# Weight split of a top-k attention and gated feed-forward kernel: high halves and half of the fractions on GpSimd, word and fraction double-buffered

## The chip, the cores and the metric

The kernel runs on one NeuronCore of a Trainium2 chip. A core has five engines, each with its own queue that it works through in order: TensorE (PE in the rows; its weight loads are PEld), VectorE (DVE), ScalarE (ACT), GpSimd (POOL) and SyncE (SP), which here issues nearly all DMAs. They wait for each other through semaphores. The metric is the time of one execution on the device in microseconds.

## The reference

```python
scores = scale * np.matmul(q, k.transpose(0, 1, 3, 2))      # 8 batches, 8 heads, 576 x 576, head 64
kth = np.partition(scores, -top_k, axis=-1)[..., -top_k:-top_k + 1]   # top_k = 32
attn = softmax(np.where(scores >= kth, scores, -1e9))
x = np.matmul(attn, v)                                       # then heads side by side: 4608 x 512
gate = 1.0 / (1.0 + np.exp(-(x @ w_gate)))                   # 512 x 1536
out = (gate * (x @ w_val)) @ w_out                           # 1536 x 512
```

All inputs and the output are float32.

## The kernel before

Attention runs as a chain of 160 steps (batch, pair of heads, tile of 128 queries). In a step TensorE makes scores into PSUM (`pss`), ScalarE copies them to SBUF (`s`), VectorE finds candidates for the 32 largest of each row (`cand`, `tops`, `leads`, many short MAX instructions), ScalarE marks what lies under a bound (`under`, one buffer), GpSimd multiplies scores and marks (`u`, L356 and L357), VectorE takes the threshold out of `u` (`kths`, L366) and masks the exponentials with it (`e`, L292, two SBUF operands). TensorE then transposes `e` and weighs the values. Of finished tokens the feed-forward part makes its products; it takes each matrix as a high part, rounded to TensorE's shorter float, and the rest, and multiplies three times.

For that the weights are split once, in the first 200 us, while the first attention steps run: `split_weights` takes 18 tiles of 128 x 1024 words. The inputs are 64-bit floats, so a tile is read as pairs of 32-bit words, `low` and `top`, each at every second word of `raw`. For each tile: two DMAs load `raw` (two buffers); ScalarE makes `lead` and `minus_zero` out of `top` (L151, L152); VectorE puts them together to a float (L153), masks sign and exponent into `top` (L161) and makes the fraction `frac` out of `low` and `top` (L162); ScalarE rounds `lead` to the high half of the weight tile (`w_split` in the rows, L163). TensorE adds up, for each half tile, `lead`, minus the high half, and `frac` (`wrest`, L168 to L170, in this order), ScalarE rounds the sum to the low half (L171), and a DMA stores the tile for later. Of these, `lead`, `frac` and `minus_zero` have one buffer each.

The order of instructions on each engine is laid out when the program is built, by a scheduler that goes by costs of its own; `run` hands it the steps and interleaves the split with them (`HELD`, `SOON`, `RUSH` say how many tiles after how many steps). On the chip the order is fixed.

Of the kernel before, what the change touches and what calls it, by code (L numbers as in the profile page):

```python
# [11 lines left out]
F32 = mybir.dt.float32  # L12
# [5 lines left out]
AF = mybir.ActivationFunctionType  # L18
ALU = mybir.AluOpType
# [11 lines left out]
def tile_topk_attention_then_gated_ffn(  # L31
# [10 lines left out]
    nc = tc.nc  # L42
# [72 lines left out]
    def split_weights():  # L115

        W = 2 * NP * P
        with ExitStack() as pre:
            signs, raws, parts = [
                pre.enter_context(tc.tile_pool(name=n, bufs=bufs, reuse_waits="tile"))  # L120
                for n, bufs in (("signs", 1), ("raw", 2), ("parts", 1))
            ]
            minus_zero = signs.tile([P, W, 2], F16, tag="minus_zero", name="minus_zero")
            nc.gpsimd.memset(minus_zero.bitcast(U32), 0)
            plus, minus = [signs.tile([P, P], F32R, tag=t, name=t) for t in ("plus", "minus")]
            nc.scalar.activation(plus, ident, AF.Copy)
            nc.scalar.activation(minus, ident, AF.Copy, scale=-1.0)
            todo = [x for g in range(NG) for x in (*range(g * FG, (g + 1) * FG), NF + 2 * g, NF + 2 * g + 1)]
            raw_of = {}

            def load_raw(idx):
                raw = raw_of[idx] = raws.tile([P, W, 2], U32, tag="raw", name=f"wraw_{idx}")
                for i in range(2):
                    half = slice(i * NP * P, (i + 1) * NP * P)
                    nc.sync.dma_start(raw[:, half].rearrange("p n t -> p (n t)"), w[idx][:, half].bitcast(U32))

            for idx in todo[:2]:
                load_raw(idx)
                yield
            for idx in todo:  # L140
                wt = pools["w"].tile([P, 2, 2, NP, P], F32R, tag="w", name=f"w_split_{idx}")
                if idx not in raw_of:
                    load_raw(idx)
                raw = raw_of.pop(idx)
                low, top = raw[:, :, 0], raw[:, :, 1]
                high, rests = [wt[:, :, x].rearrange("p i c n -> p i (c n)") for x in range(2)]
                lead = parts.tile([P, W], F32, tag="lead", name=f"wt_lead_{idx}")
                frac = parts.tile([P, W], F32R, tag="frac", name=f"wt_frac_{idx}")
                lead_u, sign = lead.bitcast(U32), top.bitcast(F32)
                with tc.issue_after(copies[1].ins):  # L150
                    nc.scalar.activation(lead, sign, AF.Copy, scale=2.0**-112)  # L151
                    nc.scalar.activation(minus_zero[:, :, 1], sign, AF.Copy, scale=2.0**-60)  # L152
                nc.vector.scalar_tensor_tensor(  # L153
                    lead_u,
                    lead_u,
                    3,
                    minus_zero.rearrange("p n t -> p (n t)").bitcast(U32),
                    op0=ALU.logical_shift_left,
                    op1=ALU.bitwise_or,
                )  # L160
                nc.vector.tensor_scalar(top, lead_u, 0xFF800000, None, op0=ALU.bitwise_and)  # L161
                nc.vector.scalar_tensor_tensor(frac, low, 2.0**-52, sign, op0=ALU.mult, op1=ALU.mult)  # L162
                nc.scalar.activation(high, lead.rearrange("p (i n) -> p i n", i=2), AF.Copy)  # L163
                yield
                for i in range(2):
                    half = slice(i * NP * P, (i + 1) * NP * P)
                    rest = ps_f.tile([P, NP * P], F32, tag="f", name=f"wrest_{idx}_{i}")
                    nc.tensor.matmul(rest, ident, lead[:, half], start=True, stop=False)  # L168
                    nc.tensor.matmul(rest, minus, high[:, i], start=False, stop=False)
                    nc.tensor.matmul(rest, plus, frac[:, half], start=False, stop=True)  # L170
                    nc.scalar.activation(rests[:, i], rest, AF.Copy)  # L171
                nc.sync.dma_start(w_split[idx], wt.rearrange("p i a c n -> p i a (c n)").bitcast(F32))
                if idx not in (*range(FG), NF, NF + 1):
                    fresh[idx] = wt
                yield
        pools["kraw"] = ctx.enter_context(tc.tile_pool(name="bkr2", bufs=2, reuse_waits="tile"))
        pools["ql"] = ctx.enter_context(tc.tile_pool(name="bql", bufs=3, reuse_waits="tile"))
        pools["x"] = ctx.enter_context(tc.tile_pool(name="bxc", bufs=NP, reuse_waits="tile"))
        pools["spare"] = ctx.enter_context(tc.tile_pool(name="late", bufs=1, reuse_waits="tile"))
# [337 lines left out]
    def run(general):  # L517
# [27 lines left out]
        if not general:  # L545
            ffn_pools()
            splits = split_weights()
# [176 lines left out]
```

## Time and profile before

| | |
|---|---|
| median of 3 runs | 1561.76 us (1561.25 to 1561.87) |
| profiled execution | 1560.76 us, its span 1558.9 us |
| busy share of the span | TensorE 97%, VectorE 84%, ScalarE 72%, GpSimd 65% |
| 18 weight tiles split | first instruction at 7.3 us, last store issued at 202.7 us |

The span is the time from the first to the last instruction of the profile; 1.86 us of the execution lie around it. A row of a group gives a count, the group's busy time, the mean length of one in ns, and the engine's idle time just before them with what ended it.

### The profile page before, as it was taken

The numbers are of one execution on the slowest core, as the hardware profiler recorded it, in microseconds if no ns is written. First come the engines' busy times: TensorE is split into PE (matmuls) and PEld (weight loads), VectorE is DVE, ScalarE is ACT, GpSimd is POOL, SyncE is SP. The second block draws the span as 40 slices with busy tenths as digits, with TensorE's granted clock in tenths as the row PEclk, the third lists the DMA queues.
The fourth block names the chain that finished last, engine by engine and source line by source line (L and its number), as shares of the span: only waits on it lengthen the run. The fifth ranks groups of instructions, "written<-read, shape, count | busy, mean of one in ns | idle before, by whom it ended". The sixth has DMA issues, their size and how long they took to land.

```text
span 1558.9 us, 33891 instructions
## 1 busy us (share of the span) xinstructions
PE 1514.1 (97%) x10586; PEld 1381.1 (89%) x10586; DVE 1310.2 (84%) x5966; ACT 1115.2 (72%) x2405; POOL 1019.9 (65%) x1596
## 2 busy tenths in 40 slices
PE   6889999999999999999999999999999999999998
PEld 2447689989999999999999999999999999999998
DVE  8999969989998889888988898998988798998311
ACT  8998968778776777777676777777766677777221
POOL 4556658877766766787566886788655786666211
PEclk9899999999999999999999999999999999999999
DMA  7663698877655665566655665565655565565574
GB/s 264 250 239 123 214 366 319 285 255 274 236 190 206 247 213 189 193 223 216 218 193 193 236 220 197 190 236 209 211 207 179 211 224 203 179 215 184 192 275 158
DMA packets 88895, 344.14 MB, mean 221 GB/s; under 512 B 9856, under 2 KB 36992, under 8 KB 57984
## 3 DMA queue, kind: packets, MB, share of 16 engines
q1 hardware_dynamic: 88560, 341.58, 61.8%
q8 instruction: 86, 1.41, 0.4%
q14 instruction: 105, 0.86, 0.2%
q10 hardware_dynamic: 144, 0.29, 0.0%
HBM read 313.52 MB, written 28.31 MB: 219 GB/s over the span
## 4 chain that ended last, share of the span: by engine, by line
PE 79%; DVE 10%; POOL 5%; ACT 2%; issue 2%; DMA 1%; POOLq 0%; DVEq 0%; ACTq 0%
PE pz L476 12%; PE pz L475 12%; PE pz L477 12%; PE pss L239 9%; PE pt L378 6%; PE po L414 6%; PE po L498 6%; PE po L497 6%; PE po L496 6%; DVE cand L338 2%; POOL u L356 2%; DVE e L292 2%; PE po L428 2%; DVE kths L366 2%; PE po L424 1%
## 5 line engine op out<-in xcount | busy, mean ns | idle before, releaser
L356 POOL TENSOR_TENSOR u<-s,under 128x288 f32<-128x288 f32 x576 | 451.5, 806 | 140.9 <-ACT under L350 132.2
L338 DVE MAX8 cand<-s 128x8 f32<-128x72 f32 x2304 | 350.7, 217 | 72.6 <-ACT s L246 64.5
L476 PE MATMUL pz<-xl,w 128*128 128x384 f32 (+1 forms) x1184 | 389.9, 330 | 1.4 <-POOL xl L448 1.4
L475 PE MATMUL pz<-xh,w 128*128 128x384 f32 (+1 forms) x1184 | 391.1, 332 | 0.0
L477 PE MATMUL pz<-xh,w 128*128 128x384 f32 (+1 forms) x1184 | 388.9, 329 | 0.0
L292 DVE SCALAR_TENSOR_TENSOR e<-s,kths,e 128x576 f32<-128x576 f32 x288 | 279.7, 976 | 5.6 <-ACT e L287 5.3
L350 ACT ACTIVATE under<-s,leads 128x576 bf16<-128x576 f32 x288 | 223.3, 776 | 75.5 <-DVE leads L342 35.7
L287 ACT ACTIVATE e<-s,st 128x576 f32<-128x576 f32 x288 | 210.1, 773 | 57.5 <-POOL st L346 56.7
L366 DVE MAX8 kths<-u 128x8 f32<-128x584 f32 x288 | 218.8, 760 | 32.8 <-POOL u L357 30.8
L483 POOL TENSOR_TENSOR gl<-gf,gh 128x384 fp32r<-128x384 f32 (+1 forms) x156 | 155.6, 998 | 123.2 <-ACT gh L482 117.0
L476 PEld LDWEIGHTS pz<-xl,w 128*128 128x128 f32 x1184 | 223.7, 189 | 2.5 <-POOL xl L448 2.2
L477 PEld LDWEIGHTS pz<-xh,w 128*128 128x128 f32 x1184 | 223.6, 189 | 0.3
L475 PEld LDWEIGHTS pz<-xh,w 128*128 128x128 f32 x1184 | 222.8, 189 | 0.8 <-issue 0.4
L379 ACT ACTIVATE et<-pt 128x384 f32<-128x384 f32 x384 | 176.7, 487 | 36.3 <-PE pt L378 34.6
L497 PE MATMUL po<-gl,w 128*128 128x384 f32 (+1 forms) x592 | 194.4, 329 | 0.6 <-POOL gl L483 0.5
L498 PE MATMUL po<-gh,w 128*128 128x384 f32 (+1 forms) x592 | 194.8, 330 | 0.0
L496 PE MATMUL po<-gh,w 128*128 128x384 f32 (+1 forms) x592 | 194.5, 333 | 0.1
L378 PE MATMUL pt<-ident,e 128*128 128x128 f32 x1152 | 176.6, 275 | 3.3 <-DVE e L292 2.0
L246 ACT ACTIVATE s<-pss 128x576 f32<-128x576 f32 x252 | 161.3, 640 | 22.0 <-PE pss L239 20.9
L239 PE MATMUL pss<-k,qh 128*128 128x288 f32 (+2 forms) x588 | 166.2, 301 | 1.9 <-ACT s L246 1.7
L239 PE MATMUL pss<-k,ql 128*128 128x288 f32 (+2 forms) x588 | 159.8, 294 | 0.0
L378 PEld LDWEIGHTS pt<-ident,e 128*128 128x128 f32 x1152 | 140.6, 141 | 17.5 <-issue 3.9
(108 smaller groups left out, 2901.9 us busy)
## 6 DMA issues: line engine op xcount, KB each, us to landing
w<-ws SPq DMA_DIRECT2D x222, 1024.0 KB, 4.9
v<-in_v_dram SPq DMA_DIRECT2D x68, 352.0 KB, 3.1
wraw<-in_w_dram SPq DMA_DIRECT2D x36, 512.0 KB, 4.5
ws<-w_split SPq DMA_DIRECT2D x18, 1024.0 KB, 4.3
qraw<-in_q_dram SPq DMA_DIRECT2D x140, 128.0 KB, 2.9
kraw<-in_k_dram SPq DMA_DIRECT2D x56, 288.0 KB, 4.5
out_dram<-acc SPq DMA_DIRECT2D x40, 192.0 KB, 5.1
out_dram<-acc SPq DMA_DIRECT2D x12, 128.0 KB, 5.5
```

Of the source, the lines that this page charges most:

```text
L239: nc.tensor.matmul(ps[:, half, o : o + n], x[:, h * P : (h + 1) * P], ks[h][:, k0 : k0 + n], start=t == 0, stop=t == len(todo) - 1,)
L292: nc.vector.scalar_tensor_tensor(e[:, j], s[:, j], kth[j], e[:, j], op0=ALU.is_ge, op1=ALU.mult, accum_out=st[:, 4 + j : 5 + j])
L338: nc.vector.max(cand[:, j, 8 * g : 8 * g + 8], s[:, j, g * SEG : (g + 1) * SEG])
L356: nc.gpsimd.tensor_tensor(u[:, j, part], s[:, j, part], under[:, j, part], op=ALU.mult)
L366: nc.vector.max(kths[:, n_tiles - col - j : n_tiles - col - j + 8], u[:, j])
L378: nc.tensor.transpose(pt[:, c], ef[:, k0 : k0 + P], ident)
L475: nc.tensor.matmul(ps, wt[:, u, 0, d], xh, start=d == 0, stop=False)
L476: nc.tensor.matmul(ps, wt[:, u, 0, d], xl, start=False, stop=False)
L477: nc.tensor.matmul(ps, wt[:, u, 1, d], xh, start=False, stop=d == NP - 1)
L496: nc.tensor.matmul(ps, wt[:, e % 2, 0, f], gh, start=f == 0, stop=False)
L497: nc.tensor.matmul(ps, wt[:, e % 2, 0, f], gl, start=False, stop=False)
L498: nc.tensor.matmul(ps, wt[:, e % 2, 1, f], gh, start=False, stop=f == FG - 1)
```

## The change

The rounding of `lead` to the high half moves from ScalarE to GpSimd, for all 18 tiles. For every second tile of the order in `todo`, the fraction is made in two instructions: ScalarE turns `low` into a scaled float in its own place (`part`), and GpSimd multiplies it by `sign`; VectorE has no part in it. `lead` and `frac` get two buffers. Lines behind the edit stand 8 further on in the rows of the changed kernel (L171 is L179 there, L292 is L300, L356 is L364), and the remaining fraction on VectorE is L167.

```diff
-                for n, bufs in (("signs", 1), ("raw", 2), ("parts", 1))
+                for n, bufs in (("signs", 1), ("raw", 2), ("parts", 2))
...
                 nc.vector.tensor_scalar(top, lead_u, 0xFF800000, None, op0=ALU.bitwise_and)
-                nc.vector.scalar_tensor_tensor(frac, low, 2.0**-52, sign, op0=ALU.mult, op1=ALU.mult)
-                nc.scalar.activation(high, lead.rearrange("p (i n) -> p i n", i=2), AF.Copy)
+                if todo.index(idx) % 2:
+                    part = low.bitcast(F32)
+                    nc.scalar.activation(part, low, AF.Copy, scale=2.0**-52)
+                    nc.gpsimd.tensor_tensor(frac, part, sign, op=ALU.mult)
+                else:
+                    nc.vector.scalar_tensor_tensor(frac, low, 2.0**-52, sign, op0=ALU.mult, op1=ALU.mult)
+                if True:
+                    nc.gpsimd.tensor_copy(high, lead.rearrange("p (i n) -> p i n", i=2))
+                else:
+                    nc.scalar.activation(high, lead.rearrange("p (i n) -> p i n", i=2), AF.Copy)
```

The scheduler lays out all five queues anew. Names in the rows below carry the step (tile and pair of heads) or a number of the build. First GpSimd's queue at the sixth weight tile, one of those with the fraction on GpSimd; before:

```order
L356 TENSOR_TENSOR u_0_1_394<-s_0_1_208,under_0_1_395 128x288 x2
L346 TENSOR_SCALAR st_0_2_626<-tops_0_2_625 128x2
L356 TENSOR_TENSOR u_0_1_394<-s_0_1_208,under_0_1_395 128x288 x2
L357 TENSOR_TENSOR u_0_1_394<-wanted,sums_0_1_392 128x2x8
L356 TENSOR_TENSOR u_1_1_497<-s_1_1_284,under_1_1_498 128x288 x4
L357 TENSOR_TENSOR u_1_1_497<-wanted,sums_1_1_495 128x2x8
L448 TENSOR_TENSOR xl_0_593<-rs_1_0_606,xh_0_592 128x256
L356 TENSOR_TENSOR u_0_2_629<-s_0_2_380,under_0_2_630 128x288 x4
L357 TENSOR_TENSOR u_0_2_629<-wanted,sums_0_2_627 128x2x8
```

And now, at the same attention steps:

```order
L169 CAST w_split_677<-wt_lead_681 128x2x512
L306 COPY inv_0_1_543<-st_0_1_392 128x128
L165 TENSOR_TENSOR wt_frac_682<-wraw_678 128x1024
L364 TENSOR_TENSOR u_0_2_631<-s_0_2_381,under_0_2_632 128x288 x2
L354 TENSOR_SCALAR st_1_2_732<-tops_1_2_731 128x2
L364 TENSOR_TENSOR u_0_2_631<-s_0_2_381,under_0_2_632 128x288 x2
L365 TENSOR_TENSOR u_0_2_631<-wanted,sums_0_2_629 128x2x8
```

The rounding (CAST, L169) and the fraction (L165) stand in the queue between the attention's tasks; `u_0_2` and the `st` after it come behind them.

VectorE's queue from this tile's mask (L161) on; before:

```order
L161 TENSOR_SCALAR wraw_676<-wt_lead_679 128x1024
L338 MAX cand_0_3_858<-s_0_3_615 128x8 x2
L344 MATCH_REPLACE cand_1_2_727<-tops_1_2_728,cand_1_2_727 128x64
L338 MAX cand_0_3_858<-s_0_3_615 128x8
L344 MATCH_REPLACE cand_1_2_727<-tops_1_2_728,cand_1_2_727 128x64
L366 MAX kths<-u_0_2_629 128x8
L338 MAX cand_0_3_858<-s_0_3_615 128x8
L295 TENSOR_SCALAR st_1_1_494<-st_1_1_494 128x2
L162 SCALAR_TENSOR_TENSOR wt_frac_680<-wraw_676 128x1024
```

And now:

```order
L161 TENSOR_SCALAR wraw_678<-wt_lead_681 128x1024
L374 MAX kths<-u_1_1_499 128x8
L352 MATCH_REPLACE cand_1_2_730<-tops_1_2_731,cand_1_2_730 128x64
L346 MAX cand_0_3_862<-s_0_3_617 128x8 x4
L350 MAX tops_1_2_731<-cand_1_2_730 128x8
L346 MAX cand_0_3_862<-s_0_3_617 128x8 x4
L448 TENSOR_TENSOR rs_1_0_608<-po_1_0_596,rs_1_0_608 128x256
L374 MAX kths<-u_1_1_499 128x8
L300 SCALAR_TENSOR_TENSOR e_1_1_498,st_1_1_496<-s_1_1_284,kths,e_1_1_498 128x576
```

The fraction (L162) is gone behind the mask of this tile; other searches for maxima and the masking `e_1_1` follow instead.

ScalarE's queue around the same tile; before:

```order
L163 ACTIVATE w_split_554<-wt_lead_558 128x2x512
L152 ACTIVATE minus_zero<-wraw_676 128x1024
L447 ACTIVATE xh_0_592<-rs_1_0_606 128x256
L270 ACTIVATE s_1_2_483<-pss_1_2_1_488 128x2x288
L151 ACTIVATE wt_lead_679<-wraw_676 128x1024
L379 ACTIVATE et_0_1_698<-pt_0_1_0_699 128x3x128
L350 ACTIVATE under_0_2_630,sums_0_2_627<-s_0_2_380,leads 128x576 x2
L171 ACTIVATE w_split_554<-wrest_0_566 128x512
L171 ACTIVATE w_split_554<-wrest_1_571 128x512
```

And now:

```order
L358 ACTIVATE under_1_1_500,sums_1_1_497<-s_1_1_284,leads 128x576
L151 ACTIVATE wt_lead_681<-wraw_678 128x1024
L152 ACTIVATE minus_zero<-wraw_678 128x1024
L164 ACTIVATE wraw_678<-wraw_678 128x1024
L278 ACTIVATE s_0_3_617<-pss_0_3_0_618 128x2x288
L387 ACTIVATE et_0_1_701<-pt_0_1_0_702 128x3x128
L179 ACTIVATE w_split_556<-wrest_0_568 128x512
L179 ACTIVATE w_split_556<-wrest_1_573 128x512
L444 ACTIVATE rs_1_0_608<-po_1_0_596 128x256
```

The rounding L163 is gone from the queue, and the float of the fraction (L164) follows the two copies out of `raw`.

## Rows read from the trace of the kernel before

**Rows 1.** The page's second part: busy tenths in 40 slices of 39 us.

```profile
PE   6889999999999999999999999999999999999998
...
DVE  8999969989998889888988898998988798998311
...
POOL 4556658877766766787566886788655786666211
```

**Rows 2.** Busy time by stage, microseconds and instructions; granted clock; DMA.

```profile
0.00:116.00 116.00, 86.57 (x372) 44.75 (x372) 108.82 (x453) 104.92 (x181) 57.85 (x92) 0.91 0.69 250
116.00:220.00 104.00, 97.70 (x631) 74.49 (x631) 86.22 (x334) 83.39 (x163) 59.51 (x88) 0.98 0.59 213
220.00:1440.00 1220.00, 1216.60 (x8882) 1152.06 (x8883) 1089.39 (x5123) 902.61 (x2014) 879.71 (x1390) 1.00 0.63 220
```

**Rows 3.** VectorE's groups from 0 to 116 us: count, busy, mean, idle before.

```profile
L292 DVE SCALAR_TENSOR_TENSOR e<-s,kths,e 128x576 f32<-128x576 f32 x18 | 16.1, 897 | 0.0
L162 DVE SCALAR_TENSOR_TENSOR wt_frac<-wraw 128x1024 fp32r<-128x1024 uint32 x11 | 15.2, 1384 | 0.0
L153 DVE SCALAR_TENSOR_TENSOR wt_lead<-wt_lead,minus_zero 128x1024 uint32<-128x1024 uint32 x11 | 13.9, 1266 | 0.0
...
L161 DVE TENSOR_SCALAR wraw<-wt_lead 128x1024 uint32<-128x1024 uint32 x11 | 7.7, 702 | 0.0
```

**Rows 4.** ScalarE's groups of the split, 0 to 116 us.

```profile
L151 ACT ACTIVATE wt_lead<-wraw 128x1024 f32<-128x1024 f32 x11 | 12.9, 1171 | 0.5 <-DMA wraw<-in_w_dram 0.5
...
L163 ACT ACTIVATE w_split<-wt_lead 128x1024 fp32r<-128x1024 f32 x10 | 10.8, 1083 | 2.4 <-DVE wt_lead L153 2.4
```

**Rows 5.** Waits from 0 to 205 us: total, times, longest.

```profile
PE pss L269 <- ACT s L270: 8.7, 9, 2.8
...
DVE kths L366 <- POOL u L357: 2.8, 4, 1.0
...
PE wrest L169 <- ACT w_split L163: 1.6, 2, 1.4
...
PE pz L476 <- POOL xl L448: 1.2, 1, 1.2
```

**Rows 6.** GpSimd's lines: shortest/median/longest ns; xl's first row is the whole trace, the rest to 205 us.

```profile
L448 POOL TENSOR_TENSOR xl<-rs,xh x84: 314/662/1787, 53.4 to 1468.8; 128x192 fp32r<-128x192 f32 x28, 128x64 fp32r<-128x64 f32 x20, 128x320 fp32r<-128x320 f32 x16, 128x384 fp32r<-128x384 f32 x12
...
L448 POOL TENSOR_TENSOR xl<-rs,xh x7: 718/739/1787, 53.4 to 203.7; 128x256 fp32r<-128x256 f32 x7
...
L298 POOL COPY inv<-st x18: 280/290/861, 27.4 to 203.0; 128x128 f32<-128x128 f32 x18
...
L356 POOL TENSOR_TENSOR u<-s,under x72: 722/734/1783, 14.5 to 190.6; 128x288 f32<-128x288 f32 x72
...
L357 POOL TENSOR_TENSOR u<-wanted,sums x20: 196/219/1194, 17.2 to 191.7; 128x16 f32<-128x16 f32 x16, 128x8 f32<-128x8 f32 x4
```

**Rows 7.** The same for VectorE's lines, 0 to 205 us.

```profile
L292 DVE SCALAR_TENSOR_TENSOR e<-s,kths,e x34: 787/802/1294, 20.2 to 184.5; 128x576 f32<-128x576 f32 x34
...
L153 DVE SCALAR_TENSOR_TENSOR wt_lead<-wt_lead,minus_zero x18: 1205/1214/1741, 9.7 to 195.5; 128x1024 uint32<-128x1024 uint32 x18
...
L161 DVE TENSOR_SCALAR wraw<-wt_lead x18: 666/681/1114, 12.3 to 196.8; 128x1024 uint32<-128x1024 uint32 x18
...
L162 DVE SCALAR_TENSOR_TENSOR wt_frac<-wraw x18: 1199/1214/1751, 13.0 to 197.9; 128x1024 fp32r<-128x1024 uint32 x18
```

**Rows 8.** Timeline from 44.3 to 46.9 us of both engines: start, length.

```profile
45.07 1.74 DVE L153 SCALAR_TENSOR_TENSOR wt_lead<-wt_lead,minus_zero 128x1024 uint32<-128x1024 uint32 x1
...
44.32 1.42 POOL L356 TENSOR_TENSOR u<-s,under 128x288 f32<-128x288 f32 x2
45.70 1.19 POOL L357 TENSOR_TENSOR u<-wanted,sums 128x16 f32<-128x16 f32 x1
```

**Rows 9.** GpSimd's largest group, 0 to 116 us.

```profile
L356 POOL TENSOR_TENSOR u<-s,under 128x288 f32<-128x288 f32 x40 | 35.4, 909 | 14.9 <-ACT under L350 14.7
```

## Prediction

> **What bounds the kernel now.** I first read the page's busy digits [rows 1], which show where TensorE isn't full: it stands at 9 from the fifth slice on, and only before that at 6 and 8. VectorE is at 9 in most early slices and GpSimd at 4 to 6. Then I cut the span at 116 us, where the feed-forward products begin, and at 220 us [rows 2]. From 220 to 1440 us TensorE is busy 1216.60 of 1220 us. Its work there is fixed, so the end moves with the moment at which this full stretch begins, and with little else. Up to 116 us TensorE is busy 86.57 us at a mean granted clock of 0.91, that is, part of the time at the lower of its two levels; VectorE is busy 108.82 us, nearly all that is left after its start at about 6 us, and ScalarE 104.92 us. So VectorE bounds this first stage and ScalarE is close behind. From 116 to 220 us TensorE has 6.3 us of idle time and VectorE 17.8. A microsecond gained or lost on VectorE before 116 us moves the end by about one; later it moves little.
>
> VectorE's groups of the stage [rows 3] hold what the change touches: 11 fractions (L162). ScalarE's [rows 4] hold 10 roundings (L163). The list of waits [rows 5] says who is late for whom: VectorE waits for GpSimd's `u` only 2.8 us in 205 us, TensorE for ScalarE's score copies 8.7 us.
>
> **VectorE's saving.** Of the first 11 tiles, five (second, fourth, ...) lose their fraction on VectorE: 5 × 1.384 us [rows 3] = **−6.9 us** in the stage that VectorE bounds. The four others of the later seven fall where VectorE has idle time; I count nothing for them.
>
> **The price on GpSimd.** The trace has no such instruction at this size. For the multiplication, GpSimd's subtraction `xl` takes 314 ns at its shortest, for its smallest form of 64 columns, and 718 ns for 256 [rows 6]: 2.10 ns for an element, so 0.718 + 768 × 0.0021 = 2.33 us for 1024 (an estimate). Its operands stand at every second word, which no GpSimd row shows. Lower bound: VectorE's own 1.20 us for the same operands [rows 7]; upper bound: twice the reading time, 4.7 us. I take 2.33, since on VectorE L162 with such operands is as fast as L153 mostly without (1199 and 1205 ns [rows 7]). For the rounding the nearest row is the copy L298, 290 ns for 128 columns; with a fixed part of 0.18 us (314 ns less 64 × 2.10) it comes to 0.18 + 8 × 0.11 = 1.06 us. Bounds: VectorE's mask pass at 0.67 us [rows 7] below, and the two-operand price of 2.33 us above. I take 1.06, the same operation. To 116 us GpSimd thus gets 11 × 1.06 + 5 × 2.33 = 23.3 us on top of 57.85 [rows 2].
>
> The Trainium skill ("GPSIMD Engine Reference", section "7. Performance pitfalls for Q7 kernels") gives a surcharge, from 1.9 to 2.9 cycles an element, only where the step between elements is over 8 bytes; here it is exactly 8. By that page the price would stay at 2.33 us; with the surcharge it would be about 3.5 us (an estimate from the page). No row here shows it.
>
> **What the new GpSimd work does to VectorE.** This is the term that decides. In the timeline [rows 8] VectorE's L153 starts at 45.07 us while GpSimd's `u` runs to 45.74; it takes 1.74 us where 1.21 is usual. GpSimd's next task, L357, starts at 45.70 and takes 1.19 us where 0.22 is usual [rows 6]; it ends 0.08 us after L153. Each waits for the other. The four lines that show this are the masking L292, L153, L161 and L162. Their mean over their shortest [rows 3, 7] gives what VectorE loses now: 18 × 0.110 + 11 × 0.185 + 11 × 0.061 + 11 × 0.036 = 5.1 us. A rule of thumb fits: an instruction that comes at a random moment waits, on average, the sum of d²/2 over GpSimd's tasks, divided by the time. With `u` alone, 40 tasks [rows 9] of 0.722 us [rows 6] in the 107 us from its start, that is 10.4 / 107 = 0.097 us each, for 51 instructions 5.0 us. The new tasks are longer, and d counts squared: 11 × 1.06²/2 + 5 × 2.33²/2 = 19.8, by 107 us 0.185 us each; for the 46 instructions left, **+8.5 us**. Bounds: 2 us, if GpSimd's new tasks mostly start behind VectorE's and do the waiting themselves; 15 us and more at the upper prices, where GpSimd would be full. So VectorE gains nothing in the stage: −6.9 + 8.5 = +1.6 us.
>
> **The other terms.** *ScalarE* is relieved of 10 × 1.083 and gets 5 conversions; the nearest row is L151, 1.171 us, which reads the same tile at the same step. That is −5.0 us on an engine that isn't the bound; it can shorten TensorE's 8.7 us of waits for scores [rows 5]. I take **−1 us** (0 to −4). If VectorE's cover were gone, the 5 us would count in full.
>
> *Waits on GpSimd.* The rounding waits for L153, the multiplication for L161 and ScalarE's L164. Behind them in GpSimd's queue stand `u` and `st` of the attention, as the order shows at the sixth tile; ScalarE's next `under` (one buffer) waits for `u`, and VectorE's `kths` too. GpSimd's load in the stage goes from about half to some three quarters. The new order sets `kths` far behind `u`, so I take **+2 us** for `u` (0 to 8). TensorE waits 1.6 us for the high half now and 1.2 us for `xl`, with score products queued behind; on the busier engine I add **+1 us** (0 to 5).
>
> *Two buffers* end no wait that the rows show: L162 and L153 have no idle time before them, L151 0.5 us for its DMA [rows 3, 4]. Zero. *DMAs* don't move, but `raw` of an odd tile comes free behind GpSimd's multiplication instead of VectorE's, some 2 us later; its load had that time to spare (0.5 us of wait in 11 tiles). Zero; without the spare time ScalarE's L151 would be late. *The order of all queues* is new. From 220 to 1440 us there are 3.4 us of idle time to gain and more to lose; **+0.6 us** (−2 to +4).
>
> **Sum:** −6.9 + 8.5 − 1 + 2 + 1 + 0.6 = +4.2 us. From the profiled execution's 1560.76 us that is 1565.0; the median lies 1.0 us higher, so 1566.0 us. About 0.2%, or 3.1 us, is what a measurement of this kernel can tell from no change.
>
> **Rivals.** *The saving and the blocking cancel* (same): the blocking is 4 to 5 us as it is today, since a task of GpSimd that waits for VectorE tends to start behind it, and `u` stays early enough, as the 2.8 us suggest. Then −6.9 + 5 − 1 + 2 + 1 = 0, 1562 us. Against it speaks the squared length.
>
> *Faster:* GpSimd is the one that waits. In the rows it waits longer than VectorE even now: 40 tasks at 909 ns instead of 722 lose 7.5 us [rows 6, 9], VectorE 5.1. If the added blocking falls to its lower bound of 2 us and ScalarE's relief counts 2, −6.9 + 2 − 2 + 1 = −5.9, 1556 us. It decides from the point where blocking and late `u` together stay under some 4 us in the stage.
>
> *Much slower:* the thing that both engines need is itself full. VectorE's four lines alone take 18 × 0.787 + 11 × (1.205 + 0.666 + 1.199) = 47.9 us; GpSimd's tasks without their waiting some 42 (57.85 less 2.5 of setup, 7.5 of `u`, and about 6 of the others, an estimate). That is 90 of 107 us. The change takes 6.0 from the one and adds 23.3 to the other: 107.2 of 107. If nothing may overlap, each start waits for the other engine, and queues grow as at any full server; with the upper prices of the two instructions still more. I put it at +12 us, 1574 us.
>
> By the Trainium skill ("SBUF — State Buffer", section "Who interferes with whom") this rival is the rule: a VectorE instruction with two SBUF inputs, or in a two-port mode, and a GpSimd instruction that reads SBUF exclude each other for the whole instruction. The trace agrees nearly: L153 lost 0.53 us of the 0.67 for which `u` still ran, so starts and ends overlap by some 0.13 us, and this leaves the pair a little room.
>
> **How the numbers follow.** Forecast, slightly slower (1565 to 1570 us): 0.36. Cancel: 0.32. Faster: 0.22. Much slower: 0.10. So faster 0.22, same 0.32, slower 0.46. The range leaves out the lower part of the faster case and the end of the much slower one: 1556 to 1575 us.
>
> **What the new profile would show.** Right: fractions on GpSimd near 2.3 us and roundings near 1.1 at their shortest, more at the mean; L300 and L153 above today's means; VectorE still busy nearly without a gap to the first `pz`, with that moment 2 to 5 us later than now; TensorE full from then. Wrong: means of L300 and L153 no higher than now, or the first `pz` earlier; a wait for `u` of 10 us and more; or a loss that lies behind 220 us, in the new order and not in the split.

## The result and the profile after

| | before | after |
|---|---|---|
| median of 5 runs each | 1561.87 us | 1580.16 us (1579.49 to 1584.01) |
| ratio, 95% interval | | 1.0117 (1.0103 to 1.0131) |
| profiled execution, span | 1560.76, 1558.9 us | 1580.16, 1578.2 us |

The changed kernel is 18.3 us slower. The forecast was 4.2 us slower, and the time lies outside the range: the sign was right, the size and its cause were not. The right sign is luck, as the experiments show.

TensorE's busy digits after, for [rows 1]:

```profile
PE   6789999999999999999999999999999999999998
```

The same stages as in [rows 2], after:

```profile
0.00:116.00 116.00, 85.64 (x365) 44.01 (x365) 106.36 (x435) 101.16 (x173) 78.95 (x105) 0.91 0.72 253
116.00:220.00 104.00, 97.94 (x583) 71.78 (x583) 85.33 (x320) 74.09 (x148) 67.78 (x93) 0.93 0.51 183
220.00:1440.00 1220.00, 1210.59 (x8797) 1141.68 (x8795) 1072.47 (x5081) 897.09 (x2000) 875.75 (x1383) 1.00 0.62 219
```

GpSimd took the work as planned: 78.95 us to 116 us, against a forecast of 57.85 + 23.3 = 81.2. The first stage looks nearly unchanged on TensorE (365 matmuls against 372). The loss shows in the two other rows. From 116 to 220 us TensorE is as busy as before but starts 583 matmuls instead of 631, at a clock of 0.93 instead of 0.98. From 220 to 1440 us it starts 8797 instead of 8882 and has 9.4 us of idle time instead of 3.4.

VectorE's groups to 116 us, for [rows 3]:

```profile
L300 DVE SCALAR_TENSOR_TENSOR e<-s,kths,e 128x576 f32<-128x576 f32 x18 | 17.6, 980 | 0.0
L153 DVE SCALAR_TENSOR_TENSOR wt_lead<-wt_lead,minus_zero 128x1024 uint32<-128x1024 uint32 x12 | 17.0, 1418 | 3.5 <-ACT minus_zero L152 2.4 <-issue 1.1
...
L161 DVE TENSOR_SCALAR wraw<-wt_lead 128x1024 uint32<-128x1024 uint32 x11 | 9.9, 904 | 0.0
...
L167 DVE SCALAR_TENSOR_TENSOR wt_frac<-wraw 128x1024 fp32r<-128x1024 uint32 x6 | 8.0, 1331 | 0.0
```

All but the fractions are longer than before. The new instructions, shortest, median and longest in ns, for [rows 6] and the estimates made from them:

```profile
L165 POOL TENSOR_TENSOR wt_frac<-wraw x9: 1887/1893/1894, 22.2 to 200.3; 128x1024 fp32r<-128x1024 f32 x9
L169 POOL CAST w_split<-wt_lead x18: 1027/1037/1558, 12.8 to 197.3; 128x1024 fp32r<-128x1024 f32 x18
L164 ACT ACTIVATE wraw<-wraw x9: 1119/1150/1180, 13.0 to 190.5; 128x1024 f32<-128x1024 uint32 x9
```

**Where the split loses.** The first `pz` of the feed-forward part starts at 98.6 us (98.3 before), so the mark that the prediction watched hardly moved. What moved is the input of the fourth block, ScalarE's `xh`. One row for each kernel, before and after, ScalarE's `xh` between 95 and 120 us (first and last start), and the first products `gh` of the feed-forward part:

```profile
L447 ACT ACTIVATE xh<-rs x2: 406/412/417, 100.5 to 115.6; 128x256 fp32r<-128x256 f32 x2
...
L482 ACT ACTIVATE gh<-gf x3: 412/418/419, 122.1 to 126.2; 128x256 fp32r<-128x256 f32 x3
```

```profile
L455 ACT ACTIVATE xh<-rs x2: 401/426/450, 104.5 to 119.8; 128x256 fp32r<-128x256 f32 x2
...
L490 ACT ACTIVATE gh<-gf x2: 424/430/437, 133.4 to 135.2; 128x256 fp32r<-128x256 f32 x2
```

`xh` comes 4.2 us later, `gh` 11.3 us. `xh` is rounded from `rs`, in whose making two engines take part: ScalarE copies factors for the rows out of PSUM, and VectorE multiplies `po` by them. Both steps in the timelines, before and then after:

```profile
112.61 0.36 ACT L436 ACTIVATE rs<-po 128x256 f32<-128x256 f32 x1
...
115.11 0.41 DVE L440 TENSOR_TENSOR rs<-po,rs 128x256 f32<-128x256 f32 x1
```

```profile
115.73 0.36 ACT L444 ACTIVATE rs<-po 128x256 f32<-128x256 f32 x1
...
116.89 1.33 ACT L152 ACTIVATE minus_zero<-wraw 128x1024 f16<-128x1024 f32 x1
...
119.05 0.78 ACT L358 ACTIVATE under<-s,leads 128x576 bf16<-128x576 f32 x1
...
119.83 0.40 ACT L455 ACTIVATE xh<-rs 128x256 fp32r<-128x256 f32 x1
...
119.05 0.40 DVE L448 TENSOR_TENSOR rs<-po,rs 128x256 f32<-128x256 f32 x1
```

The copy starts 3.1 us later than before, and VectorE's step 3.9 us. On ScalarE a piece of the split, `minus_zero`, and an `under` now stand between the copy and `xh`, where neither stood before. They cost `xh` little: VectorE's step ends at 119.45 us, and `xh` starts 0.38 us later. Most of the delay was there before, in ScalarE's queue ahead of the copy and in VectorE's behind it. The chain of work that ended last says the same. It leaves VectorE's queue for TensorE's feed-forward stretch at these points, before and then after:

```profile
115.55 0.43 ACT xh L447
```

```profile
129.67 0.90 PE pt L386 x3
```

In the changed kernel this chain stays on VectorE 14 us longer, and what TensorE waits for at its end is VectorE's `e`: a transposition `pt` of `e` stands in TensorE's queue ahead of the next `pz`.

TensorE stood still meanwhile, and then ran at the lower of its two levels. Busy time and clock in three stretches, before and then after:

```profile
116.00:124.00 8.00, 7.98 (x50) 6.91 (x51) 8.00 (x43) 6.94 (x16) 5.95 (x9) 0.79 0.16 59
124.00:132.00 8.00, 8.00 (x50) 5.81 (x49) 8.00 (x39) 4.88 (x12) 5.43 (x10) 1.00 0.04 11
116.00:136.00 20.00, 19.98 (x129) 15.61 (x129) 20.00 (x97) 15.82 (x35) 13.34 (x20) 0.91 0.10 35
```

```profile
116.00:124.00 8.00, 3.84 (x15) 2.04 (x16) 8.00 (x40) 5.41 (x12) 6.88 (x9) 0.70 0.28 86
124.00:132.00 8.00, 7.31 (x30) 5.52 (x30) 8.00 (x40) 6.96 (x15) 6.13 (x11) 0.50 0.16 63
116.00:136.00 20.00, 15.14 (x73) 11.43 (x74) 20.00 (x106) 16.30 (x36) 16.09 (x24) 0.66 0.18 60
```

Before, TensorE filled this stretch with 129 matmuls; after, it was busy 3.84 of 8 us, and then 7.31 of 8 us at 1.2 GHz, with 73 matmuls in all. Busy time by clock is 19.98 × 0.91 = 18.2 us before and 15.14 × 0.66 = 10.0 us after: some 8 us of full-speed work are missing in these 20 us (an estimate from these rows). The idle time is made up by 220 us, where the stage's row has 97.94 us of busy time against 97.70. The work is not: up to 220 us the changed kernel starts 365 + 583 = 948 matmuls, the one before 372 + 631 = 1003. At 0.14 us each, as between 400 and 1100 us below, the 55 missing ones are 7.7 us (an estimate that takes all shapes alike).

**Where the rest loses.** TensorE's waits from 400 to 1100 us after; for before, the same question has no row at all:

```profile
PE pz L484 <- POOL xl L456: 1.5, 2, 0.8
PE pss L247 <- ACT s L254: 1.3, 3, 0.5
PE pz L483 <- ACT gf L488: 1.0, 2, 0.5
PE pt L386 <- DVE e L300: 0.8, 2, 0.4
...
```

No tile is split any more in this stretch, and no instruction of the change runs there. Many small waits on many producers, on none of which anything was changed, point to another order; e6 tests it.

### The profile page after: what moved, and what is told of

It reads as the page before. It is cut to its first block, busy times and chain, and to the rows that moved or that the text cites. A ratio compares the mean times of both kernels' runs of the same rounds, so it can differ in the third digit from the quotient of the medians.

```text
span 1578.2 us, 33889 instructions
## 1 busy us (share of the span) xinstructions
PE 1526.4 (97%) x10586; PEld 1385.2 (88%) x10586; DVE 1302.4 (83%) x5957; ACT 1109.5 (70%) x2396; POOL 1054.2 (67%) x1623
## 4 chain that ended last, share of the span: by engine, by line
PE 70%; DVE 17%; POOL 5%; ACT 4%; issue 3%; DMA 1%; SPq 0%; POOLq 0%; ACTq 0%; DVEq 0%
PE pz L483 10%; PE pz L484 10%; PE pz L485 10%; PE pss L247 7%; PE pt L386 5%; PE po L422 5%; PE po L504 5%; PE po L505 5%; PE po L506 5%; DVE cand L346 4%; DVE e L300 4%; DVE kths L374 3%; POOL u L364 3%; PE po L436 2%; PE po L432 1%
## 5 line engine op out<-in xcount | busy, mean ns | idle before, releaser
L364 POOL TENSOR_TENSOR u<-s,under 128x288 f32<-128x288 f32 x576 | 457.6, 817 | 146.2 <-ACT under L358 133.7
L300 DVE SCALAR_TENSOR_TENSOR e<-s,kths,e 128x576 f32<-128x576 f32 x288 | 285.9, 996 | 3.2 <-ACT e L295 3.1
L386 PE MATMUL pt<-ident,e 128*128 128x128 f32 x1152 | 184.4, 278 | 15.2 <-DVE e L300 8.4
```

Of the source, the lines that this page charges most:

```text
L300: nc.vector.scalar_tensor_tensor(e[:, j], s[:, j], kth[j], e[:, j], op0=ALU.is_ge, op1=ALU.mult, accum_out=st[:, 4 + j : 5 + j])
L364: nc.gpsimd.tensor_tensor(u[:, j, part], s[:, j, part], under[:, j, part], op=ALU.mult)
L386: nc.tensor.transpose(pt[:, c], ef[:, k0 : k0 + P], ident)
```

## The experiments

Theory A puts the loss on the moved work (GpSimd's longer tasks hold VectorE up, or come late), theory B on the order of the queues that the scheduler made for it. To part them, the order was made an input of the kernel. A table `ORDER` names the instructions of each queue in the order of another kernel's build, and edges that set an order, without a semaphore, chain them; engines and buffers are chosen apart from it:

```diff
+    for engine, steps in table.items():
+        ...
+        for a, b in zip(row, row[1:]):
+            tc.add_manual_dep(ins[b], a, edge, reason="pin")
```

An instruction that stands on another engine in the two kernels goes to where the engine then stood in the profile. A mixed order takes from one kernel what had begun by 225 us, and the rest from the other:

```python
first = [c for c, s in A[e] if s < 225]
rest = [c for c, _ in B[e] if c not in first]
```

Every kernel with a written-out order has two buffers for word and fraction. The diffs show what an edit amounts to; in the runs it is set by switches of one kernel, whose lines stand further down (L292 is L333 in most of them). All twelve results, each against before on the same chip; "loss" is the difference of the medians in us. The intervals reach 0.9 to 1.7 thousandths to either side, that is 1.4 to 2.7 us, so smaller differences between two runs are not clear of noise:

| run | work | order | us | loss | ratio (95%) |
|---|---|---|---|---|---|
| e1 | before | after | 1579.08 | 17.0 | 1.0112 (1.0095 to 1.0129) |
| e2 | after | before | 1573.84 | 11.8 | 1.0077 (1.0060 to 1.0093) |
| e3 | after, not reading | after | 1576.72 | 14.7 | 1.0099 (1.0082 to 1.0116) |
| e4 | before, two buffers | scheduler's own | 1567.48 | 5.4 | 1.0037 (1.0027 to 1.0047) |
| e5 | after | split after, rest before | 1573.16 | 11.4 | 1.0079 (1.0064 to 1.0093) |
| e6 | before | split before, rest after | 1573.05 | 11.3 | 1.0075 (1.0062 to 1.0088) |
| e7 | before, two buffers | before | 1562.13 | 0.4 | 1.0002 (0.9993 to 1.0011) |
| e8 | rounding moved | scheduler's own | 1584.32 | 22.6 | 1.0147 (1.0131 to 1.0162) |
| e9 | before | split after, rest before | 1573.56 | 11.3 | 1.0071 (1.0057 to 1.0085) |
| e10 | rounding moved | before | 1568.03 | 5.8 | 1.0039 (1.0025 to 1.0052) |
| e11 | fractions moved | before | 1569.84 | 7.6 | 1.0050 (1.0036 to 1.0064) |
| e12 | after, not reading | before | 1572.28 | 10.7 | 1.0071 (1.0057 to 1.0085) |

**e1, before's work in the new order.** The edit to the changed kernel, with the new order written out:

```diff
-                    nc.gpsimd.tensor_copy(high, lead.rearrange("p (i n) -> p i n", i=2))
+                    nc.scalar.activation(high, lead.rearrange("p (i n) -> p i n", i=2), AF.Copy)
...
-                    nc.gpsimd.tensor_tensor(frac, part, sign, op=ALU.mult)
+                    nc.vector.scalar_tensor_tensor(frac, low, 2.0**-52, sign, op0=ALU.mult, op1=ALU.mult)
```

Expected: 

> Work of the kernel before (roundings on ScalarE, all fractions on VectorE, two buffers), but every queue held in the order of the changed kernel; a rounding or fraction stands where GpSimd's task started in the changed kernel's trace. Theory A, the long GpSimd tasks block VectorE and come late, and that is the loss: 1560 to 1565 us. Theory B, the scheduler's new order of all queues is the loss, whoever does the work: 1575 to 1582 us. Both in part: between, and the distance to 1580 is A's share.

Measured: 17.0 us of loss without any moved work, inside theory B's range. The order alone gives nearly all of the 18.3 us; the second buffer, which e1 has too, is free (e7).

**e2, the moved work in before's order.** The changed kernel's instructions, before's table. Expected: 

> Work of the changed kernel, but every queue held in the order of the kernel before; GpSimd's tasks are put in where ScalarE's rounding or VectorE's fraction started in its trace. Theory A: 1575 to 1585 us, since the same tasks are there. Theory B: 1560 to 1565 us.

Measured: 11.8 us, between the ranges of the two theories. The work is not free either in an order that wasn't made for it; the losses of e1 and e2 together are 28.8 us, more than the whole change costs, so they don't add up. To 116 us GpSimd waits 20.6 us for `lead` with a rounding at the head of its queue, and VectorE waits for GpSimd's `u` behind it:

```profile
DVE kths L407 <- POOL u L398: 5.2, 4, 2.1
```

Before, this wait is 0.3 us in the stage; in the changed kernel with its own order it has no row there.

**e3, GpSimd doesn't read.** High halves and the odd tiles' fractions are left out: memsets of about their length stand in their places, in the new order.

```diff
-                    nc.gpsimd.tensor_copy(high, lead.rearrange("p (i n) -> p i n", i=2))
+                    nc.gpsimd.memset(wt[:, :, 0].rearrange("p i c n -> p i (c n)").bitcast(U32), 0)
...
-                    nc.gpsimd.tensor_tensor(frac, part, sign, op=ALU.mult)
+                    nc.gpsimd.memset(frac.bitcast(U32), 0)
+                    nc.gpsimd.memset(frac.bitcast(U32), 0)
```

Expected: 

> Changed kernel in its own order; each GpSimd rounding becomes one memset of the same 1024 columns, each GpSimd fraction two, so GpSimd is as long busy (0.95 and 1.90 us for 1.04 and 1.89) and reads nothing; the weights come out as zero high halves and fractions. Theory A as blocking between VectorE and GpSimd tasks that read: the masking, L153 and L161 fall to the means of before (0.90, 1.29, 0.72 us) and the time by 5 to 10 us, to 1570 to 1575. Theory A as mere lateness of GpSimd's queue, or theory B: 1578 to 1582 us.

Measured: 1576.7 us, between the two ranges, and 3.6 us less loss than the changed kernel, which is not clear of noise. To 205 us the masking, L153 and L161 take 0.97, 1.33 and 0.90 us on the mean; they don't fall to before's 0.90, 1.29 and 0.72, as the first theory wanted. The memsets also don't wait for `lead` or `part`, so this bounds reading and those waits together.

**e4, two buffers alone.** Before's kernel with the one line of the pool, scheduled anew:

```diff
-                for n, bufs in (("signs", 1), ("raw", 2), ("parts", 1))
+                for n, bufs in (("signs", 1), ("raw", 2), ("parts", 2))
```

Expected: 

> Kernel before with two buffers for word and fraction and nothing else, laid out anew by the scheduler. Theory A: 1560 to 1563 us, as no engine does other work. Theory B: the order changes all through, and the time can land anywhere from 1560 to 1580 us; over 1566 would speak for it.

Measured: 5.4 us slower, 1.5 us above the mark that speaks for theory B, though no engine has other work. Whether buffers or order do it, e7 tells.

**e5 and e6, one half of the new order each.** The mixed orders above, e5 with the changed kernel's work, e6 with before's. Expected of e5: 

> The changed kernel's work, its order of every queue for all instructions that had begun by 225 us in its profile, and behind them the order of before. In the profiles the changed kernel's TensorE is some 8 us of matmul work behind at 220 us, and some 10 us more by 1100 us. Theory 'two places' (the split costs 8 us, the new order behind it 10 us more): 1570 us, 1567 to 1573. Rival 'all in the split' (what comes later only carries the loss on): 1578 to 1581. Rival 'all behind it' (the delay of the split is made up): 1562 to 1564.

Expected of e6: 

> The other half: before's work and before's order for all that had begun by 225 us, with two buffers for word and fraction, and behind it the order of the changed kernel. Theory 'two places': 1572 us, 1569 to 1575. Rival 'all in the split': 1561 to 1563. Rival 'all behind it': 1578 to 1581.

Measured: 11.4 and 11.3 us. e6 lies inside its range for "two places", e5 0.2 us above its own; both rivals, which put all of it in one half, fail. Together they are 4.4 us more than the whole change loses. A reason stands where the two orders of e5 meet: there TensorE has a wait that neither before nor after has, and its clock falls. The wait in e5, and the 20 us around it in before, after and e5:

```profile
PE pt L424 <- ACT et L425: 3.1, 1, 3.1
```

```profile
220.00:240.00 20.00, 19.95 (x202) 19.21 (x203) 19.23 (x100) 14.92 (x34) 15.59 (x27) 1.00 1.02 390
```

```profile
220.00:240.00 20.00, 19.81 (x169) 17.95 (x168) 10.04 (x49) 10.87 (x27) 11.68 (x20) 1.00 1.03 414
```

```profile
220.00:240.00 20.00, 16.11 (x116) 13.89 (x115) 9.51 (x59) 9.23 (x21) 10.08 (x17) 0.83 0.87 338
```

16.11 × 0.83 = 13.4 us of full-speed work against 19.95: this seam costs some 6.6 us (an estimate, from the slowest of e5's executions, 1578.4 us; how much the others lose there isn't shown). e6 has no such wait where its orders meet. So e5's 11.4 us are not all the split's. Without the seam some 5 us are left, and the 18.3 us of the whole change less e6's 11.3 leave 7.0, near the 7.7 us of missing matmuls above. The split's share is thus some 5 to 8 us, and the larger share lies behind it. The stretch from 400 to 1100 us in before, after, e5 and e6, in this order:

```profile
400.00:1100.00 700.00, 699.77 (x4979) 663.39 (x4978) 622.26 (x2895) 515.71 (x1138) 503.91 (x788) 1.00 0.61 211
```

```profile
400.00:1100.00 700.00, 693.82 (x4894) 655.00 (x4894) 613.76 (x2889) 514.20 (x1135) 499.26 (x785) 1.00 0.59 208
```

```profile
400.00:1100.00 700.00, 699.89 (x5023) 664.21 (x5023) 623.43 (x2901) 517.97 (x1143) 504.35 (x787) 1.00 0.61 211
```

```profile
400.00:1100.00 700.00, 694.23 (x4909) 654.57 (x4908) 612.74 (x2877) 510.11 (x1127) 501.70 (x783) 1.00 0.60 207
```

With before's order behind the split (e5) TensorE is full, with the new one (e6, after) it has some 6 us of idle time. It also starts 70 to 85 matmuls fewer than before, at 699.77 / 4979 = 0.14 us each some 10 to 12 us; but e5 starts 44 more, so the mix of shapes alone moves such a count by 6 us. The idle time is some half of e6's 11.3 us; where the rest goes these rows don't show.

**e7, two buffers in before's order.** e4's edit with before's table. Expected: 

> Before's work and before's order of every queue, with only the two buffers for word and fraction; the natural schedule with two buffers took 1567.5. If the buffers move the time only by the other order that comes with them: 1561 to 1563. If a second buffer itself, or the writing out of the order, costs time: 1565 to 1568.

Measured: no change (0.9993 to 1.0011), inside the first range. So neither the second buffer nor writing the order out costs time, and e4's 5.4 us come from its order alone.

**e8, rounding alone, scheduled anew.** The fractions all stay on VectorE:

```diff
-                if todo.index(idx) % 2:
+                if False:
```

Expected: 

> Part of the change alone, in the order that the scheduler then makes: GpSimd rounds every tile's high half, two buffers, and VectorE multiplies every fraction as before. By the work alone (18 GpSimd roundings of 1.04 us instead of 18 of ScalarE's, each able to hold VectorE up) it should be 1 to 4 us above before: 1563 to 1566. If the order decides, the time has nothing to do with the work that was moved and lies anywhere from 1558 to 1582; then a time above 1570 speaks for it, as the work alone can't give that.

Measured: 22.6 us, more than the whole change loses, with less work moved; in before's order the same work costs 5.8 us (e10). The time of a scheduled build says little of the work that was moved.

**e9, before's work in the split's new order.** As e5, with e1's edit. Expected: 

> As the run with the split in the new order and the rest in before's (1573.2 us), but with before's work: ScalarE rounds, VectorE multiplies every fraction, each put where the changed kernel's instruction began. If the order of the split costs the 11.4 us and the moved work nets to nothing: 1571 to 1576. If the moved work costs them (GpSimd's longer tasks hold VectorE up): 1562 to 1566.

Measured: 11.3 us, like e5's 11.4 within the intervals. In this mixed order the moved work nets to about nothing; the order costs all of it. The hole is there as well; the stretch from 116 to 136 us in e9:

```profile
116.00:136.00 20.00, 13.94 (x65) 10.28 (x66) 20.00 (x100) 15.68 (x35) 11.65 (x20) 0.66 0.21 73
```

13.94 × 0.66 = 9.2 us of full-speed work where before had 18.2, 9 us behind at 136 us. The 9 are not a share of the 11.3: part of them is made up later, as in the changed kernel, and the seam of e5 follows here too (16.12 us busy from 220 to 240 us, at a clock of 0.83).

**e10 and e11, the parts of the work in before's order.** e10 moves the 18 roundings only, e11 the 9 fractions only:

```diff
-                    nc.scalar.activation(high, lead.rearrange("p (i n) -> p i n", i=2), AF.Copy)
+                    nc.gpsimd.tensor_copy(high, lead.rearrange("p (i n) -> p i n", i=2))
```

```diff
-                    nc.vector.scalar_tensor_tensor(frac, low, 2.0**-52, sign, op0=ALU.mult, op1=ALU.mult)
+                    nc.scalar.activation(part, low, AF.Copy, scale=2.0**-52)
+                    nc.gpsimd.tensor_tensor(frac, part, sign, op=ALU.mult)
```

Expected of e10: 

> Before's order of every queue with one part of the change: GpSimd rounds all 18 high halves, put where ScalarE's rounding began; the fractions stay on VectorE; two buffers. Both parts in before's order took 1573.8 us. GpSimd waited there 20.6 us within 116 us for the tile at the head of its queue, with the softmax work behind it. Theory 'head of the queue': most of the 11.8 us come from these roundings, 1568 to 1573. Rival 'blocking by the work' (18 times 1.04 us, by the rule of the prediction 4 us of its 8.5, less ScalarE's relief): 1562 to 1566.

Expected of e11: 

> Before's order with the other part: GpSimd multiplies the 9 odd tiles' fractions (1.89 us each), ScalarE makes their floats besides its roundings, VectorE is 9 instructions lighter; two buffers. Theory 'head of the queue' (the roundings do the harm): 1561 to 1566. Rival 'the multiplications do it' (TensorE waited 5.6 us within 116 us for GpSimd's fractions): 1568 to 1573.

Measured: 5.8 and 7.6 us. e10 lies on the lower edge of "head of the queue", e11 inside its rival: the roundings are not most of e2's loss, and the fractions are not harmless. Both parts cost, with 13.4 us together a little more than e2.

**e12, waits without reading, in before's order.** As e2, but each new GpSimd instruction handles one column, which still waits for its tile, and memsets fill the time; high halves and odd fractions are left out.

```diff
+                    nc.gpsimd.tensor_copy(high[:, :, :1], lead.rearrange("p (i n) -> p i n", i=2)[:, :, :1])
+                    nc.gpsimd.memset(wt[:, :, 0].rearrange("p i c n -> p i (c n)").bitcast(U32), 0)
...
+                    nc.gpsimd.tensor_tensor(frac[:, :1], part[:, :1], sign[:, :1], op=ALU.mult)
+                    nc.gpsimd.memset(frac.bitcast(U32), 0)
+                    nc.gpsimd.memset(frac.bitcast(U32), 0)
```

Expected: 

> Before's order of every queue and the changed kernel's division of the work, as in the run that took 1573.8 us, but GpSimd reads next to nothing: each rounding and each multiplication is made of one column, which waits for the same tile, and of memsets of the same length (0.98 us for a high half, twice 0.98 us for a fraction). The high halves and the odd tiles' fractions are left out (zero). Theory 'blocking' (GpSimd's reading holds VectorE up, the term of 8.5 us in the prediction): 1563 to 1567. Rival 'late by its place' (the pieces wait at the head of GpSimd's queue and come late, read or not): 1571 to 1575. Half and half: 1568 to 1570.

Measured: 10.7 us of loss against 11.8 in e2, a difference inside the intervals. VectorE's masking and its mask pass (L161 before) to 205 us, first in e2, then in e12:

```profile
L333 DVE SCALAR_TENSOR_TENSOR e<-s,kths,e 128x576 f32<-128x576 f32 x34 | 36.3, 1068 | 0.0
...
L193 DVE TENSOR_SCALAR wraw<-wt_lead 128x1024 uint32<-128x1024 uint32 x17 | 13.5, 796 | 0.0
```

```profile
L336 DVE SCALAR_TENSOR_TENSOR e<-s,kths,e 128x576 f32<-128x576 f32 x34 | 30.7, 902 | 0.0
...
L193 DVE TENSOR_SCALAR wraw<-wt_lead 128x1024 uint32<-128x1024 uint32 x17 | 15.5, 909 | 0.0
```

The masking is no longer held up (902 ns, as before's 898), and yet nearly the whole loss stays. Not all of the blocking is gone: the mask pass takes 909 ns, before 721, which is 3.2 us over its 17 instructions. VectorE's wait for `u` to 116 us is 7.2 us here, against 5.2 in e2. So "late by its place" fits, and its range holds the time: in before's order the new tasks stand in front of `u` and cost by their length, read or not.

Which of the queues behind 220 us loses the 11.3 us wasn't tried: one engine's queue of the new order among the others of the old one doesn't fit together, since each waits for what the other hasn't reached. None of the runs is faster than before.

## Why the prediction was wrong

**The failed step** is "the order of all queues is new", counted at +0.6 us (−2 to +4). With no work moved, the new order costs 17.0 us (e1): 11.3 behind the split (e6), and some 5 to 8 in it (e5 and e9 without their seam, and what e6 leaves of the whole). The bound was drawn from idle time seen from 220 us on, as if an order could lose only a little there and nothing in the split. What the prediction named last as a sign against it, "a loss that lies behind 220 us, in the new order and not in the split", is the larger half of what came; the rest came from the order inside the split.

**The sentence on the path failed with it:** "a microsecond gained or lost on VectorE before 116 us moves the end by about one". VectorE's busy time before 116 us fell by 2.5 us, the first `pz` came 0.3 us later where 2 to 5 were forecast, and yet TensorE's long stretch began some 11 us later. VectorE does stand on the path, until 129.7 us in the changed kernel. But what moves the end is where in its queue, and in ScalarE's, the steps stand that TensorE waits for (`rs` and `xh`, 4.2 us later, then `e`), and the lower clock that TensorE ran at after its idle stretch; the amount of VectorE's work is not the measure.

**VectorE's saving** (−6.9 us): the five fractions left as counted; its busy time to 116 us went from 108.82 to 106.36. But 3.5 us of idle time came in before L153, 2.4 of them for ScalarE's `minus_zero`, which had no term.

**GpSimd's prices.** Rounding 1.04 us at the median (1.06 forecast). Multiplication 1.89 us (2.33), that is 1.85 ns for an element where `xl` gave 2.10: the step of two words costs nothing on top that these rows show, and the price carried over from `xl` was too high. The Trainium skill ("GPSIMD Engine Reference", "7. Performance pitfalls for Q7 kernels") has its surcharge only at a longer step, and these rows agree.

**Blocking** (+8.5 us) was real, and a third to a half as large. By the same reckoning, means over the shortest of [rows 7], VectorE now loses 18 × 0.193 + 12 × 0.213 + 11 × 0.238 + 6 × 0.132 = 9.4 us against 5.1: +4.3. But part of this comes with the order and without the moved work. The same four lines in e1:

```profile
L333 DVE SCALAR_TENSOR_TENSOR e<-s,kths,e 128x576 f32<-128x576 f32 x18 | 17.7, 984 | 0.0
L185 DVE SCALAR_TENSOR_TENSOR wt_lead<-wt_lead,minus_zero 128x1024 uint32<-128x1024 uint32 x11 | 15.0, 1360 | 1.9 <-ACT minus_zero L184 1.9
L200 DVE SCALAR_TENSOR_TENSOR wt_frac<-wraw 128x1024 fp32r<-128x1024 uint32 x11 | 13.6, 1239 | 0.0
L193 DVE TENSOR_SCALAR wraw<-wt_lead 128x1024 uint32<-128x1024 uint32 x11 | 8.3, 753 | 0.0
```

They lose 18 × 0.197 + 11 × 0.155 + 11 × 0.040 + 11 × 0.087 = 6.6 us, so the moved work adds 2.8. And it is worth little in the end: without reading the loss shrinks by 1.1 us (e12 against e2) or by 3.6 (e3, without the waits as well), neither clear of noise. The rival "much slower" came near in its time (1574) and falls by its mechanism, as e1 takes 1579 us with no work moved. The rule that it drew from the Trainium skill ("SBUF — State Buffer", "Who interferes with whom") is seen here from VectorE's side: the longest masking, 2429 ns where 791 is the shortest, started at 200.4 us, just behind GpSimd's last multiplication at 200.3.

**Late `u`** (+2 us): in the new order VectorE has no such wait to 116 us; in before's order 5.2 us (e2). **The high half and `xl`** (+1 us): TensorE has no wait for GpSimd's high half or for `xl` to 205 us, so this came to nothing as well. **ScalarE** (−1): not seen; TensorE waits 9.7 us for score copies to 205 us instead of 8.7. **Two buffers** (zero): right (e7).

Two readings were off, without a part in the sum. TensorE's digits before stand at 9 from the fourth slice on, not the fifth, and the feed-forward products begin at 98.3 us, not at 116. And of the inputs only `q`, `k` and `v` are float32; the weights are 64-bit floats, which is why the split reads pairs of words.

**The rival "cancel" was right about the net of the work, not about each term, and wrong about the time.** In the order that the scheduler made for it, the moved work nets to 1.3 us (the changed kernel against e1) or 0.1 us (e5 against e9), neither clear of noise. It is one order against the other that decides: the forecast added up work and left the order as a small remainder.

## What to carry to other kernels

Where a scheduler lays out the queues, an edit changes two things, the work and the order, and the second can be the larger: here a second buffer that costs nothing moved the time by 5.4 us through the order alone. Write the order out as an input before judging an edit, and test the old work in the new order and the new work in the old one. Where two orders are joined, look at the seam for waits that neither has alone. In a kernel bound by one full engine, look at where in the other queues that engine's next inputs are made, and at its clock right then, and not only at how busy the feeding engine is.

## What was not expected of the hardware

GpSimd's multiplication never got longer: nine took 1887 to 1894 ns, while its rounding went from 1027 to 1558 and VectorE's masking up to 2429:

```profile
L300 DVE SCALAR_TENSOR_TENSOR e<-s,kths,e x33: 791/948/2429, 28.2 to 200.4; 128x576 f32<-128x576 f32 x33
```

So of this pair the one that waited was VectorE. And TensorE, after it had been busy 11.53 of 16 us (12.82 before) and then 3.84 of 8, ran at 1.2 GHz just when its long stretch of feed-forward work began; the row of before and then of after:

```profile
100.00:116.00 16.00, 12.82 (x85) 8.37 (x82) 16.00 (x72) 14.84 (x31) 11.15 (x15) 1.00 0.59 203
```

```profile
100.00:116.00 16.00, 11.53 (x76) 7.29 (x75) 16.00 (x64) 15.99 (x31) 9.80 (x14) 1.00 0.76 274
```

Before, TensorE also ran at the lower level for a part of the stretch from 116 us (a mean clock of 0.79 to 124 us), but from 124 to 132 us it was at full speed, where the changed kernel was at half.

A `pz` of the same form took 0.28 us ahead of the fall and 0.41 us behind it; start and length from TensorE's timeline:

```profile
112.19 0.28 PE L485 MATMUL pz<-xh,w_split 128*128 128x256 f32 x1
...
126.13 0.41 PE L485 MATMUL pz<-xh,w_split 128*128 128x256 f32 x1
```
